# VectorE's written order held two statements longer, to the end of batch 1's first sums

## The chip, the cores and the metric

The kernel runs on one NeuronCore of one Trainium2 chip. Its time is device time of one execution in microseconds (us), and a kernel's time is the median of several executions. A core has TensorE (PE in the profile; its weight loads stand apart as PEld), VectorE (DVE), ScalarE (ACT), GpSimd (POOL) and SyncE (SP), which issues the DMAs here. Each engine works through its own list of instructions in order and waits on semaphores for the others. DVE, ACT and POOL read and write SBUF, PE reads SBUF and writes PSUM, which has 8 banks of 512 float32 per partition.

## What is computed

Everything is float32. Eight batches of 512 tokens, 8 heads of 64, and 32 state rows per head:

```
scores  = x @ state^T / 8;  a  = softmax(scores);   xread = a @ state
scores2 = state @ x^T / 8;  a2 = softmax(scores2);  sread = a2 @ x
y = concat(xread, sread) over tokens            # 544 rows per batch, 512 wide
out = elu(y @ w_in) @ w_out                      # 512 -> 2048 -> 512
```

## The kernel before

**Stages.** A batch's 512 tokens are handled as four 128-row blocks. `batch(b)` (line 847) runs, for `b` from 1 to 7, in two stretches. First come 16 rounds of the first layer: `ffn1` (PE, two matmuls into a bank) and `elu` (two ACT passes, then one DVE instruction that writes `g_all[:, fo]`). Then comes the second layer, `g_all` times `w_out`, as a Strassen product of 2 by 2 blocks (line 572) with seven products. Product P1 is a11 by b11, P2 is a12 by b21. P6, P7 and P5 follow, and two more products are split once more into seven smaller ones (`Second`, line 513). a11 and a12 are the even and odd 128-wide pieces of `g_all` for the first 256 tokens, a21 and a22 those for the other 256.

**Sums.** `whole.sums()` (line 589) is four DVE instructions on 128x1024 elements: two write a21 = a11 - a21 (profile name `g_all<-g_all`), two write s = a22 - a21 (`s<-g_all`). P6 is the first product that reads s, P7 the first that reads the new a21. P1 and P2 read neither.

**The next batch's attention is woven in.** During the last four rounds DVE turns the tokens of batch b+1 (`turn_blocks`, four 128x512 transposes `xT_b<-x_blocks`). After P1's first half PE computes the scores from them and two blocks of `make_m` (`ps<-xT_b,kT`, `ps<-w_in,kT`); DVE, ACT and POOL then do both softmaxes (`attention`, line 709; the first DVE instruction is `top<-ps`). `move_state` (line 359) makes two DVE transposes `a_blocks<-a_s` and then 16 DMAs `aT_s<-a_blocks` of 32 KB from SP. `state_read` (line 374; PE, `ps<-x_sb,aT_s`) needs all of them. It stands in PE's order after the first half of P7. Behind the 16 DMAs SP has two loads of `w_in` and the load of a later batch's tokens.

**Batch 1 alone** also has `weight_sum` in every second round: sums of `w_out` blocks (`t_w<-...`, `w_out<-w_out`, 128x1024), which the Strassen products need. `Second.weights` (line 520) forms further sums of 128x512 (`t<-t_w`, `t_w<-t_w`, `w_out<-w_out`, `w_in<-...`; `t` is the profile's short name for the tile of `second[4]`). They come as hooks after later steps.

**What sets the order.** A scheduler orders each engine's instructions, with estimates of when their inputs are there. The class `InOrder` (line 94) overrides this: while its `on` is true, an instruction issued through it is pinned behind everything issued before it on that engine; while it is false, the scheduler places it. PE and SP are always held. ACT and POOL are held through the first batch. VectorE is held until `vector.on = False` (line 864), which `batch` reaches first in batch 1 and which nothing turns on again. All engine calls go through this helper, so the profile gives one line, L100, for nearly everything, and instructions are told apart by tiles.

Of the kernel before, what the change touches and what calls it, by code (L numbers as in the profile page):

```python
# [25 lines left out]
def kernel(  # L26
# [67 lines left out]
    class InOrder:  # L94
# [10 lines left out]
    tensor, sync, vector, scalar, gpsimd = (  # L105
        InOrder(e) for e in (nc.tensor, nc.sync, nc.vector, nc.scalar, nc.gpsimd)
    )
# [25 lines left out]
    def load_x(b, engines):  # L133
        x_t[b] = xpool.tile([P, R, DM], FP32, name="x_sb")
        x_v = x[b].rearrange("h (p r) d -> p r h d", r=R)
        for r in range(R):
            engines[r % len(engines)].dma_start(
                out=x_t[b][:, r].rearrange("p (h d) -> p h d", d=D), in_=x_v[:, r]
            )

    def load_blocks(b):

        for i in range(2):
            st[b, "blocks", i] = raw = opool.tile([P, 2, R * P], FP32, tag="o", name="x_blocks")
            for j in range(2):
                for k in range(4):
                    x_v = x[b, 2 * (2 * i + j) + k // 2].rearrange(
                        "(q p r) d -> p r q d", q=P // 32, r=R  # L150
                    )
                    sync.dma_start(
                        out=raw[k * 32 : (k + 1) * 32, j].rearrange(
                            "p (r q d) -> p r q d", r=R, d=32
                        ),
                        in_=x_v[:, :, :, k % 2 * 32 : (k % 2 + 1) * 32],
                    )

    def turn_blocks(b, m):

        i, j = divmod(m, 2)
        if j == 0:
            st[b, "xT", i] = work.tile([P, 2, R * P], FP32, tag="w", name="xT_b")
        st[b, m] = st[b, "xT", i][:, j]
        vector.transpose(st[b, m], st[b, "blocks", i][:, j])
# [244 lines left out]
    def fetch_w_in(c, k):  # L410

        for i in range(2):
            sync.dma_start(
                out=w_in[:, 2 * (k + i) : 2 * (k + i) + 2],
                in_=w_in_mem[:, 2 * (c + i) : 2 * (c + i) + 2],
            )

    def make_m(b, c, h=None, first=6):

        c_in = c if b < 2 else c % 2  # L420
        halves = slice(2 * c_in, 2 * c_in + 2) if h is None else slice(2 * c_in + h, 2 * c_in + h + 1)
        assert h is None or b == 0
        st[b, "m", c] = by_state(b, [w_in[:, halves, m] for m in range(NP)], first)

    def copy_m(b, c, g, copy):
        if g == 0:
            m_t[b, c] = mpool.tile([P, G, 512], FP32, name="m_sb")
        copy(out=m_t[b, c][:, g], in_=st[b, "m", c][:, g])
# [20 lines left out]
    def elu(ps, fo):  # L449

        max_part(fo, exp_part(ps), ps)

    def ffn1(b, fo):


        ps = bank(4 + fo % 2 if b == 0 else 3 + (fo + 1) % 3)
        for k in range(G):
            matmul(
                ps,
                m_t[b, fo // 4][:, k, fo % 4 * P : (fo % 4 + 1) * P],  # L460
                st[b, k, "aT"],
                start=(k == 0),
                stop=(k == G - 1),
            )
        return ps
# [37 lines left out]
    def weight_sum(i, half):  # L503

        if i != 3 and half == 0:
            t_w[i] = [
                work.tile([P, FO // 4, DM // 2], FP32, tag="w", name="t_w") for k in range(2)
            ]
        x, y = {1: (b12, b11), 2: (b22, t_w.get(1)), 3: (b22, b12), 4: (b21, t_w.get(2))}[i]
        k = slice(half, half + 1)  # L510
        combine(t_w[i][k], x[k], y[k])
# [197 lines left out]
    def attention(b):  # L709


        def both(*fs):
            for g in range(G):
                for f in fs:
                    f(b, g)

        def s1():

            scores(b)
            for c in range(2):  # L720
                make_m(b, c, first=4 - 2 * c)
            both(column_max, turn_scores, column_exp, row_max, row_subtract, row_exp)
            both(row_sum, row_scale, column_total)
            for c in range(2):
                for g in range(G):
                    copy_m(b, c, g, (scalar.copy, vector.tensor_copy)[g])

        def s2():
            both(turn_tokens)
            move_state(b)  # L730

        nop = lambda: None
        return [lambda: (s1(), s2()), nop, nop, nop, nop, nop, lambda: (state_read(b), keep_read(b))]

    def store(b, i, o_sb):
        rows = out_b[b, 0:S].rearrange("(p r) c -> p r c", r=R)
        sync.dma_start(out=rows[:, 2 * i : 2 * i + 2], in_=o_sb)
# [109 lines left out]
    def batch(b):  # L847
        if b + 1 < B:
            load_blocks(b + 1)
        for fo in range(FO):  # L850
            elu(ffn1(b, fo), fo)
            if fo > 11 and b + 1 < B:
                turn_blocks(b + 1, fo - 12)
            if fo == FO // 4 + 1:
                for c in (2, 3):
                    make_m(b, c, first=6 if c == 2 else 0)
            if FO // 4 + 1 <= fo < FO // 4 + 5:
                c, g = divmod(fo - FO // 4 - 1, G)
                copy_m(b, 2 + c, g, vector.tensor_copy)
            if b == 1 and fo % 2 == 1:  # L860
                weight_sum((1, 2, 4, 3)[fo // 4], fo % 4 // 2)
            if b > 1 and fo == FO // 4 + 2:
                fetch_w_in(0, 0)
        vector.on = False
        nxt = b + 1 < B
        hooks = attention(b + 1) if nxt else [turn_read]
        if nxt and b > 0:
            s1 = hooks[0]
            hooks[0] = lambda: (s1(), fetch_w_in(2, 0))
        if b + 2 < B:  # L870
            hooks += [lambda: load_x(b + 2, [sync])]
        if b == 1:
            hooks += [lambda: second[4].weights(t_w[4]), lambda: second[3].weights(b22)]
            hooks += [lambda: second[5].weights(t_w[1]), lambda: second[7].weights(t_w[3])]
            used = {k: second[k] for k in (4, 3)}
        else:
            used = second
        whole = Strassen(2, used)
        whole.sums()
        for f in whole.steps():  # L880
            f()
            if hooks:
                hooks.pop(0)()
        if not nxt:
            fetch_w_in(2, 2)
        for i in (1, 0):
            store(b, i, whole.o_sb[i])
# [28 lines left out]
    for b in range(1, B):  # L916
        batch(b)
# [31 lines left out]
```

## Time and profile before

| | |
|---|---|
| median of 7 executions | 746.92 us (746.16 to 749.46) |
| the profiled execution | 749.46 us, of which the span is 747.6 us |
| granted TensorE clock | 1.000 |
| PE busy | 723.5 us, 97% |
| DVE busy | 486.1 us, 65% |
| ACT busy | 293.8 us, 39% |
| HBM read and written | 59.24 MB and 13.11 MB |

The profile is of one execution. In its rows "ps<-w_out,g_all 128x256" is an instruction that writes `ps` from `w_out` and `g_all`; "x16" says how many neighbours were merged. Brackets give the idle time of that engine just before and what ended it. Batch 1's first layer ends at about 162 us, its second layer at about 215 us.

### The profile page before, as it was taken

The page shows a single profiled execution, that of the slowest core. Times are in us where ns is not written, and L with a number is a line of the kernel's source. Part 1 is how long each engine was busy: PE and PEld are TensorE (multiplying, and loading weights), DVE is VectorE, ACT ScalarE, POOL GpSimd, SP SyncE. Part 2 cuts the span into 40 slices and gives each one's busy share as a digit, 9 for nine tenths or more (in the row PEclk, how much of TensorE's full clock was granted, in tenths as well). Part 3 has the DMA queues.
Part 4 walks back from the last instruction along what each step waited for, and adds up shares of the span by engine and source line. Part 5 has one row for each costly group of instructions (what it writes and reads, how often), then busy time and mean ns, then how long its engine had stood idle before and what let it go on. Part 6 is the DMA issues. An engine that isn't in the chain of part 4 may idle for free.

```text
span 747.6 us, 11377 instructions
## 1 busy us (share of the span) xinstructions
PE 723.5 (97%) x4472; PEld 502.3 (67%) x4472; DVE 486.1 (65%) x892; ACT 293.8 (39%) x539; POOL 34.4 (5%) x38
## 2 busy tenths in 40 slices
PE   3899999999999999999999999999999999999998
PEld 1634444347874799459944896479746894699886
DVE  1999984699537783677656873787367745556331
ACT  3899974552126410651045213621164106500420
POOL 0200002002000200011000200020002000000000
PEclk9999999999999999999999999999999999999999
DMA  9566910701634053603551154307350403004000
GB/s 282 188 208 223 319 48 1 159 11 17 182 84 142 1 164 90 169 1 80 147 131 67 24 175 106 119 11 188 82 145 1 142 29 140 1 1 141 29 4 25
DMA packets 126366, 76.25 MB, mean 102 GB/s; under 512 B 113768, under 2 KB 114280, under 8 KB 122472
## 3 DMA queue, kind: packets, MB, share of 16 engines
q1 hardware_dynamic: 124004, 74.90, 34.5%
q10 hardware_dynamic: 2308, 0.62, 0.4%
q8 instruction: 35, 0.57, 0.3%
q14 instruction: 19, 0.16, 0.1%
HBM read 59.24 MB, written 13.11 MB: 97 GB/s over the span
## 4 chain that ended last, share of the span: by engine, by line
PE 89%; DVE 5%; DMA 2%; SPq 1%; ACT 1%; issue 1%; POOL 0%; ACTq 0%; DVEq 0%; POOLq 0%
PE ps L100 89%; SPq L100 1%; DMA x_sb<-in_x_dram 1%; DVE w_in L100 1%; DVE g_all L100 1%; DMA raw<-in_moe_w_out_dram 0%; DVE top L100 0%; DVE s L100 0%; DVE w_out L100 0%; ACT e_sb L100 0%; DVE total_t L100 0%; POOL t_sb L100 0%; ACT xT L100 0%; DVE xT_b L100 0%; DVE aT L100 0%
## 5 line engine op out<-in xcount | busy, mean ns | idle before, releaser
L100 PE MATMUL ps<-w_out,g_all 128*128 128x256 f32 (+2 forms) x1088 | 232.5, 366 | 1.6 <-DVE o_sb L100 0.8
L100 PE MATMUL ps<-aT,m_sb 128*128 128x512 f32 x512 | 226.3, 595 | 1.1 <-DVE m_sb L100 0.8
L100 PEld LDWEIGHTS ps<-w_out,g_all 128*128 128x128 f32 x1088 | 176.6, 191 | 54.0 <-issue 37.1
L100 PEld LDWEIGHTS ps<-aT,m_sb 128*128 128x128 f32 x512 | 95.4, 190 | 122.0 <-issue 109.1
L100 ACT ACTIVATE e_sb<-ps 128x512 f32<-128x512 f32 (+1 forms) x144 | 82.6, 573 | 219.9 <-PE ps L100 204.7
L100 DVE SCALAR_TENSOR_TENSOR g_all<-e_sb,ps 128x512 f32<-128x512 f32 (+1 forms) x144 | 94.3, 657 | 101.0 <-ACT e_sb L100 100.4
L100 DVE TENSOR_TENSOR o_sb<-o_sb,ps 128x128 f32<-128x128 f32 (+2 forms) x170 | 52.7, 310 | 75.2 <-PE ps L100 73.5
L100 ACT ACTIVATE e_sb<-e_sb 128x512 f32<-128x512 f32 (+1 forms) x144 | 87.6, 608 | 4.6
L100 PE MATMUL ps<-t_w,s 128*128 128x256 f32 (+1 forms) x480 | 88.8, 339 | 0.0
L100 PEld LDWEIGHTS ps<-t_w,s 128*128 128x128 f32 x480 | 77.6, 191 | 8.1 <-DVE o_sb L100 0.2
L100 ACT COPY o_sb<-ps 128x512 f32<-128x512 f32 (+2 forms) x52 | 20.6, 424 | 152.2 <-PE ps L100 144.5
L100 ACT ACTIVATE raw<-raw 128x512 f32<-128x512 uint32 x64 | 43.8, 685 | 1.0
L100 DVE TENSOR_TENSOR s<-s,g_all 128x512 f32<-128x512 f32 (+1 forms) x36 | 32.2, 897 | 15.9 <-PE ps L100 15.5
L100 POOL TENSOR_TENSOR t_sb<-t_sb,top_t 128x512 f32<-128x512 f32 x16 | 16.7, 1048 | 519.7 <-DVE top_t L100 519.7
L100 DVE TENSOR_TENSOR g_all<-g_all,s 128x512 f32<-128x512 f32 (+1 forms) x36 | 32.1, 892 | 9.6 <-PE ps L100 9.6
L100 PE MATMUL ps<-w_in,kT 64*32 64x512 f32 (+1 forms) x576 | 34.0, 547 | 1.1 <-ACT a_s L100 1.1
L100 DVE TENSOR_TENSOR g_all<-g_all 128x512 f32<-128x512 f32 (+1 forms) x36 | 32.2, 895 | 0.5
L100 DVE TENSOR_TENSOR s<-g_all 128x512 f32<-128x512 f32 (+1 forms) x36 | 31.6, 883 | 1.1 <-DMA aT_s<-a_blocks 0.8
L100 PE MATMUL ps<-t_w,g_all 128*128 128x128 f32 (+1 forms) x240 | 32.1, 282 | 0.0
L100 PE MATMUL ps<-w_in,s 128*128 128x128 f32 x240 | 31.2, 277 | 0.0
L100 PEld LDWEIGHTS ps<-t_w,g_all 128*128 128x128 f32 x240 | 29.8, 192 | 0.5
L100 PEld LDWEIGHTS ps<-w_in,s 128*128 128x128 f32 x240 | 28.7, 192 | 0.6 <-DVE o_sb L100 0.3
(86 smaller groups left out, 557.0 us busy)
## 6 DMA issues: line engine op xcount, KB each, us to landing
w_in<-w_in_mem SPq DMA_DIRECT2D x26, 1024.0 KB, 6.0
raw<-in_moe_w_in_dram SPq DMA_DIRECT2D x16, 512.0 KB, 4.8
raw<-in_moe_w_out_dram SPq DMA_DIRECT2D x16, 512.0 KB, 4.2
out_dram<-o_sb SPq DMA_DIRECT2D x16, 512.0 KB, 2.9
x_sb<-in_x_dram SPq DMA_DIRECT2D x30, 256.0 KB, 4.7
x_blocks<-in_x_dram SPq DMA_DIRECT2D x96, 64.0 KB, 2.4
w_in_mem<-w_in SPq DMA_DIRECT2D x4, 1024.0 KB, 8.4
aT_s<-a_blocks SPq DMA_DIRECT2D x96, 32.0 KB, 1.9
```

The source lines that it names most:

```text
L100: ins = getattr(self.engine, name)(*args, **kw)
```

## The change

`vector.on = False` moves from the end of the rounds to behind `whole.sums()`. Between the two places VectorE is issued nothing but the four sums, since the hooks and products are only set up there. So in batch 1 the four sums are pinned behind all that was issued on VectorE before them: the last `elu`, the last transpose, the last `weight_sum`. In later batches `vector.on` is false already. The instructions are the same; only places in the order differ.

```diff
@@ def batch(b)
             if b > 1 and fo == FO // 4 + 2:
                 fetch_w_in(0, 0)
-        vector.on = False
         nxt = b + 1 < B
         hooks = attention(b + 1) if nxt else [turn_read]
         if nxt and b > 0:
@@
             used = second
         whole = Strassen(2, used)
         whole.sums()
+        vector.on = False
         for f in whole.steps():
             f()
             if hooks:
```

The built order of VectorE's instructions at this place, before and changed (sizes are elements per partition):

```
before                              changed
(round 8)                           (round 8)
g_all<-g_all     1024               -
...                                 ...
xT_b<-x_blocks    512  first        xT_b<-x_blocks    512  first
-                                   t<-t_w,t          512
elu of round 13                     elu of round 13
xT_b<-x_blocks    512  second       xT_b<-x_blocks    512  second
w_out<-w_out     1024               w_out<-w_out     1024
elu of round 14                     elu of round 14
xT_b<-x_blocks    512  third        xT_b<-x_blocks    512  third
elu of round 15                     elu of round 15
g_all<-g_all     1024               t<-t_w,t          512
s<-g_all         1024 x2            t_w<-t_w          512
t<-t_w,t          512               w_out<-w_out      512
                                    w_in<-w_out       512
xT_b<-x_blocks    512  fourth       xT_b<-x_blocks    512  fourth
w_out<-w_out     1024               w_out<-w_out     1024
-                                   g_all<-g_all     1024 x2
-                                   s<-g_all         1024 x2
top<-ps (softmax begins)            top<-ps (softmax begins)
...                                 ...
a_blocks<-a_s     512 x2            a_blocks<-a_s     512 x2
```

Between `top` and the second `a_blocks` the order is the same. Behind it, the small weight sums that stood there before are gone where they were moved forward, and `o_sb<-o_sb,ps` of P2 stands before the last `aT` transpose. On ACT the second copy `m_sb<-ps` moves ahead of the first softmax step and the copy of P1's result (`o_sb<-ps`) ahead of the second. The orders of PE, POOL and SP are unchanged.

## The prediction

> **What bounds the kernel now.** I read the page's busy times first, then the chain of work that ended last, then the timelines of PE, DVE and SP around the end of batch 1's rounds, where alone the order changes.
>
> ```profile
> PE 723.5 (97%) x4472; PEld 502.3 (67%) x4472; DVE 486.1 (65%) x892; ACT 293.8 (39%) x539; POOL 34.4 (5%) x38
> ```
>
> PE is busy 97%, so time is won or lost only where PE is held up. The chain shows where that happens in batch 1:
>
> ```profile
> 163.09 0.62 DVE xT_b L100
> 163.71 1.70 DVE g_all L100 x2
> 165.42 0.07 DVE s L100
> ...
> 166.47 1.22 DVE s L100
> 167.69 0.60 DVE t L100
> 168.29 0.63 DVE xT_b L100
> 168.92 0.04 issue
> 168.97 400.46 PE ps L100 x2596
> ```
>
> Before 168.97 the chain lies on DVE: sums and a small weight sum stand ahead of the fourth `xT_b`, without which the last scores cannot start. From there PE runs 400 us without a hold. PE's timeline gives the hold, and the place where the softmax's result is needed next:
>
> ```profile
> 165.56 1.07 PE L100 MATMUL ps<-xT_b,kT 64*32 64x512 f32 x12
> 168.97 0.62 PE L100 MATMUL ps<-xT_b,kT 64*32 64x512 f32 x2 [2.33 <-DVE xT_b L100]
> ...
> 171.66 10.63 PE L100 MATMUL ps<-w_out,g_all 128*128 128x256 f32 x48
> 182.12 7.07 PE L100 MATMUL ps<-t_w,s 128*128 128x256 f32 x32
> 189.03 3.62 PE L100 MATMUL ps<-w_out,g_all 128*128 128x256 f32 x16
> 192.58 1.10 PE L100 MATMUL ps<-x_sb,aT_s 128*32 128x64 f32 x64
> ```
>
> PE idles 2.33 us for `xT_b`. At 192.58 `state_read` starts with no idle time. Its input arrives just before, as SP and DVE show:
>
> ```profile
> 179.13 0.66 DVE L100 STREAM_TRANSPOSE a_blocks<-a_s 128x512 f32<-128x512 f32 x1
> ...
> 192.58 0.69 DVE L100 TENSOR_TENSOR s<-g_all 128x512 f32<-128x512 f32 x1 [0.83 <-DMA aT_s<-a_blocks]
> ```
>
> ```profile
> 179.85 10.43 SPq L100 DMA_DIRECT2D aT_s<-a_blocks  x16
> 190.38 1.03 SPq L100 DMA_DIRECT2D w_in<-w_in_mem  x2
> ```
>
> SP issues the 16 transfers from 179.85 to 190.28, 0.06 us behind the last `a_blocks` (179.79). At a median of 1.9 us to landing the last is there at 192.18. A DVE sum that waits for the same transfers starts at 192.58. So `state_read` has 0 to 0.4 us of slack, against about 3 us in batch 2 (issue ends 271.09, landed 273.0, `state_read` at 276.12). That is what the change works on.
>
> **The change part by part.** Starts on DVE follow each other by 0.60 us for 128x512, 0.63 behind a transpose, 1.13 for 128x1024 (163.63, 164.21, 165.34, 167.60, 168.20 in DVE's timeline).
>
> *Round 8: a sum of 1.13 us goes.* It stood at 148.90 in a stretch where DVE ran behind ACT; by 156.65 before and changed meet again, since that `elu` waits for ACT until 156.61. PE does not idle between 149.04 and 165.56. Worth 0, hidden by PE's own work.
>
> *Round 13: a 128x512 sum comes in* at 159.61. The next `elu` starts at 160.21 instead of 160.08; the rest of the 0.60 fills an idle 0.39 and a wait. The last `elu` slips from 163.63 to 163.76. P1's first half (162.02 to 165.56) reads up to round 14, the eighth of its matmuls at about 163.6, and that `elu` ends at 163.2. No cost.
>
> *Ahead of the fourth transpose* three sums of 1.13 and one of 0.60 go, 3.99 us; four of 0.60 come, 2.40. The transpose starts at 163.76 + 0.58 + 2.40 = 166.74 instead of 168.20, so PE resumes 1.46 us sooner, at 167.51. This gain is PE's until `state_read`: P1's second half, P2, P6 and half of P7 need nothing that is late. P6's s is ready at 173.0 and P6 starts at 180.66; ACT copies P1's bank at about 175.1, behind the first softmax step, with P1 done at 173.74.
>
> *Behind the fourth transpose*, ahead of `top`, now stand the `w_out` sum (1.10) and all four sums (4.52): 166.74 + 0.63 + 1.10 + 4.52 = 172.99, against 170.04. So the softmax starts 2.95 us later although PE's scores are there sooner.
>
> *The softmax itself is as before.* From `top` to the end of the second `a_blocks` it took 9.75 us (170.04 to 179.79), and 9.75 again in batch 2 (250.87 to 260.62). ACT's and POOL's steps hang on DVE's and move with them. `a_blocks` ends at 182.74.
>
> *SP, all 16 DMAs counted:* 0.06 to start, 10.43 to issue, 1.9 to land: 195.13. PE starts between there and 0.4 later, by the slack above; I take 195.33, the middle. PE is at `state_read` at 192.58 - 1.46 = 191.12, idles 4.2 us and starts 2.75 us later than before. The two `w_in` loads behind the transfers and the token load, which waits for `state_read`, move with it; batch 2 reads them tens of us later.
>
> *Work behind `state_read`.* DVE reaches P2's `o_sb` sum at 182.74 and frees the bank by 183.4; P7 needs it at 187.57. The two sums that P5 needs end at about 191; P5 would start at 200. The small weight sums moved forward no longer stand behind `a_blocks`. So DVE makes no second hold, and little can be won back: from 192.58 on PE's only idle time is 0.81 us (at 594.64, for `o_sb`). Were all of it to go, the sum would be 1.9 us.
>
> *The clock after a longer idle stretch* is not shown by the trace. Bounds: no cost as after 2.33 us idle, where the next 48 matmuls took 10.63 us, 0.221 each, as do the 32 at 182.12; or as in the start of the kernel, after sparse work:
>
> ```profile
> 16.46 1.96 PE L100 MATMUL ps<-xT,kT 64*32 64x512 f32 x16 [1.67 <-ACT xT L100]
> 18.35 4.69 PE L100 MATMUL ps<-ident 128*128 128x128 f32 x28
> ```
>
> The same 16 scores take 1.09 us in batch 2 and 28 such `ident` matmuls 3.39 us at 30.97, so 0.87 + 1.30 = 2.2 us were lost, with a granted clock of 1.00 in both places. I take 0, since the gap lies in dense work, nearer to the first row; 2.2 stays the upper end.
>
> [...]
>
> **Sum:** -1.46 + 4.2 = +2.75 us. The profiled execution would go from 749.46 to 752.2. It is the slowest of the seven shown, 2.54 over the median, so for the median I add the same to 746.92: 749.7 us.
>
> **Rivals.**
> 1. *The clock drops after the idle stretch.* For it: the two slow rows above; against it: 2.33 us did nothing. 746.92 + 2.75 + 2.2 = 751.9 us.
> 2. *The gain stays: faster.* `state_read` is not held, because `aT_s` lands by 191.1. The softmax would have to start by 168.9, that is, the 5.62 us of sums behind the transpose would have to delay it by nothing. It decides above a landing of 192.6. For it: all that PE needs up to there is early. Against it: DVE works in order, and every step up to the landing has a row. 746.92 - 1.46 = 745.5 us.
> 3. *No change.* The loss meets the gain, if the chain from `top` to `state_read` has over 2 us that can shrink, for instance in ACT's and POOL's waits. Against it: 9.75 us in two batches alike, and 16 equal issues of 0.65. 746.9 us. That the change does nothing is excluded by the built order.
> 4. *A second hold on DVE*, such as P2's `o_sb` sum releasing P7's bank late. It would need over 4 us more delay than I find; every us beyond costs one. 750.7 us for one.
>
> **How the numbers follow.** Forecast 0.65, clock 0.17, faster 0.06, no change 0.07, second hold 0.05. The forecast's own range is 748.8 (1.9 us) to 749.9 (2.95 us). For 8 in 10 I leave out the faster case and part of the unchanged one and go up past the clock case; the seven executions alone spread over 3.3 us, so the range is 747.8 to 752.6. A change under 0.2% (1.5 us) cannot be told from none in this kernel. Faster 0.06; same 0.08 (no change, and a small part of the forecast won back); slower 0.86.
>
> **What would show it.** In the changed profile PE's idle time before the last scores falls from 2.33 to about 0.9 us; `top` starts at about 173.0; `a_blocks` ends at about 182.7; `state_read` shows an idle time of about 4.2 us put down to `aT_s<-a_blocks` and starts at about 195.3; P7's second half behind it keeps 0.22 us per matmul (slow clock: 0.4). The prediction is wrong if `top` still starts near 170, if `state_read` has no idle time before it, or if 2 us are won back after it.

## The result, and the profile after

The changed kernel is slower. Its median is 751.52 us (17 executions, 748.09 to 752.46), against 748.1 us for the kernel before in the same comparison (45 executions). The ratio is 1.004, with a 95% interval of 1.003 to 1.005: about +3.0 us, where +2.75 was predicted (the two medians themselves lie 3.4 us apart). The profiled execution of after took 750.23 us with a span of 748.4 us and a mean granted clock of 0.995; the one of before took 749.46 with a span of 747.6 and a clock of 1.000.

The two profiles cannot be subtracted as they stand, since after reached batch 1's P1 2.36 us earlier (159.66 instead of 162.02) by differences in work that the change does not touch: its first scores, behind the start-up loads, already begin at 13.58 instead of 16.46. So I count from the start of P1's first half in batch 1 to the start of the same half in batch 2. That took 84.10 us before (162.02 to 246.12) and 87.58 after (159.66 to 247.24): +3.48 us. The same interval of batches 2 to 5 is equal to within 0.02 us (79.59, 79.75, 79.53, 79.67 after). All of the loss is in batch 1. From batch 2's P1 to the end after took 0.3 us less than before (748.4 - 247.24 against 747.6 - 246.12), with PE's one wait for `o_sb` in that stretch down from 0.8 to 0.5 us.

PE's busy time, from the page of after, grew by 3.5 us with the same number of matmuls, so some of them ran slower:

```profile
PE 727.0 (97%) x4472; PEld 505.2 (68%) x4472; DVE 485.2 (65%) x892; ACT 294.3 (39%) x539; POOL 34.4 (5%) x38
```

The chain of waits of after, between 159 and 195 us (start, duration, what):

```profile
164.42 0.62 DVE xT_b L100
165.04 1.10 DVE w_out L100
166.15 2.27 DVE g_all L100 x2
168.42 2.27 DVE s L100 x2
170.69 0.60 DVE top L100
...
179.76 0.59 DVE a_blocks L100
180.40 0.63 SPq L100
...
189.58 0.61 SPq L100
190.24 1.91 DMA aT_s<-a_blocks
192.14 0.14 issue
192.28 3.04 PE ps L100 x60
```

Before, this chain left DVE at the fourth `xT_b` and then ran on PE for 400 us. Now it goes on along DVE, through the four held sums into the softmax, then through SP's 16 issues and the last landing, and comes to PE only with `state_read`. The duration of the DMA in the chain, 1.91 us, is counted from the start of the last issue at 190.24.

PE's timeline of after shows both ends of the trade:

```profile
163.20 1.08 PE L100 MATMUL ps<-xT_b,kT 64*32 64x512 f32 x12
165.10 0.62 PE L100 MATMUL ps<-xT_b,kT 64*32 64x512 f32 x2 [0.82 <-DVE xT_b L100]
...
185.17 3.62 PE L100 MATMUL ps<-w_out,g_all 128*128 128x256 f32 x16
188.71 0.31 PE L100 MATMUL ps<-x_sb,aT_s 128*32 128x64 f32 x4
189.67 0.27 PE L100 MATMUL ps<-x_sb,aT_s 128*32 128x64 f32 x2 [0.65 <-DMA aT_s<-a_blocks]
192.28 1.88 PE L100 MATMUL ps<-x_sb,aT_s 128*32 128x64 f32 x58 [2.34 <-DMA aT_s<-a_blocks]
194.09 4.36 PE L100 MATMUL ps<-w_out,g_all 128*128 128x256 f32 x16
198.28 7.07 PE L100 MATMUL ps<-t_w,s 128*128 128x256 f32 x32
```

The hold ahead of the last scores fell from 2.33 to 0.82 us. In exchange `state_read` waits twice, 0.65 and 2.34 us. Six of its 64 matmuls run as the first blocks land, and the other 58 wait for the last. Behind the wait the work is slower than before: those 58 take 1.88 us (all 64 took 1.10 before), and the 16 matmuls of P7's second half take 4.36 us instead of 3.72.

The table of stretches says why (columns: stretch, its length, busy time and count of PE, PEld, DVE, ACT and POOL, the granted PE clock, the DMA share, GB/s). After:

```profile
180.00:190.00 10.00, 9.29 (x47) 7.68 (x45) 9.14 (x12) 0.59 (x1) 0.96 (x1) 1.00 0.26 43
190.00:195.00 5.00, 2.72 (x60) 2.49 (x61) 1.99 (x3) 0.63 (x2) 0.00 (x0) 0.70 0.70 211
195.00:196.00 1.00, 1.00 (x5) 0.82 (x5) 0.00 (x0) 0.00 (x0) 0.00 (x0) 0.79 0.95 361
196.00:200.00 4.00, 4.00 (x20) 3.52 (x19) 1.38 (x2) 0.59 (x1) 0.00 (x0) 1.00 1.09 321
```

The granted clock is 0.50 from 192.0, still inside the wait, to 195.4 us (the finer stretches are shown at the end). In the profile of before it is 1.00 throughout batch 1. So two things were added: a wait, and a slow clock behind it.

Steps of the two kernels, counted from the start of P1's first half (162.02 before, 159.66 after), in us:

| step | before | after | difference | predicted |
|---|---|---|---|---|
| last scores resume | 6.95 | 5.44 | -1.51 | -1.46 |
| `top` starts | 8.02 | 10.94 | +2.92 | +2.95 |
| second `a_blocks` ends (start of SP's first issue less 0.06) | 17.77 | 20.68 | +2.91 | +2.95 |
| `state_read` (its bulk) starts | 30.56 | 32.62 | +2.06 | +2.75 |
| P7's second half starts | 31.59 | 34.43 | +2.84 | +2.75 |
| P5 starts | 35.15 | 38.62 | +3.47 | +2.75 |

Up to SP the prediction holds to 0.05 us. Then `state_read` starts 0.7 us sooner than predicted, and the slow clock takes that back and 0.7 us more.

### The profile page after: what moved, and what is told of

Read it like the earlier page. It is cut to its first block, busy times and chain, and to the rows that moved or that the text cites. A ratio compares the mean times of both kernels' runs of the same rounds, so it can differ in the third digit from the quotient of the medians.

```text
span 748.4 us, 11377 instructions
## 1 busy us (share of the span) xinstructions
PE 727.0 (97%) x4472; PEld 505.2 (68%) x4472; DVE 485.2 (65%) x892; ACT 294.3 (39%) x539; POOL 34.4 (5%) x38
## 4 chain that ended last, share of the span: by engine, by line
PE 80%; DVE 12%; SPq 3%; ACT 2%; DMA 1%; issue 1%; POOL 0%; ACTq 0%; DVEq 0%; POOLq 0%
PE ps L100 80%; DVE w_in L100 4%; DVE w_out L100 3%; SPq L100 3%; DVE g_all L100 2%; DMA x_sb<-in_x_dram 1%; DVE top L100 1%; DVE s L100 1%; DMA aT_s<-a_blocks 1%; ACT e_sb L100 0%; DVE t_sb L100 0%; POOL t_sb L100 0%; DVE m_sb L100 0%; DVE top_t L100 0%; DVE t_w L100 0%
```

## The experiments

The theory by now: the gain at the last scores is real (1.5 us), the four sums ahead of `top` delay `aT_s`, and `state_read` waits for it. The clock part (rival 1) and the wait are to be told apart. The rivals to be excluded: that the loss comes from something else that moved, such as the small weight sums, and that the slow clock is an accident of one execution. The first four kernels share their executions of before, whose median there was 747.87 us.

**The wait filled with matmuls.** On the changed kernel, PE is given 13 `ident` matmuls (26 in the profile) ahead of `state_read`, so that it does not idle. Their result is not used.

```diff
+        if b == 1:
+            read_hook = hooks[6]
+            def warm_read():
+                for _ in range(13):
+                    matmul(bank(4)[:, :P], ident, ident, start=True, stop=True)
+                read_hook()
+            hooks[6] = warm_read
```

> The changed kernel with 13 products of the identity with itself (26 matmuls on PE, into a bank nobody reads) ahead of batch 1's state_read, in the time in which PE would wait for aT_s. Theory: the loss has two parts, a later state_read (2.1 us) and a slow clock behind the idle stretch (about 1 us on average, 1.4 us in the profiled execution). Then the filled kernel keeps the first part alone: state_read's bulk starts as late as before relative to P1, the granted clock is 1.00 from 190 us on, P7's second half takes 3.6 us instead of 4.36, ratio to the kernel before about 1.0028 instead of 1.004. Rival (the slow stretch is an accident of that execution, the stall alone is the loss): ratio unchanged at 1.004.

Measured: 749.28 us (748.38 to 750.38), ratio 1.0021 [1.0011, 1.0032]. PE's timeline of this kernel:

```profile
188.26 3.06 PE L100 MATMUL ps<-ident 128*128 128x128 f32 x26
191.25 0.31 PE L100 MATMUL ps<-x_sb,aT_s 128*32 128x64 f32 x6
191.92 1.05 PE L100 MATMUL ps<-x_sb,aT_s 128*32 128x64 f32 x58 [0.36 <-DMA aT_s<-a_blocks]
192.90 3.72 PE L100 MATMUL ps<-w_out,g_all 128*128 128x256 f32 x16
```

The last block lands when it did before the fill: the 58 matmuls start 32.62 us after P1 (191.92 less 159.30), exactly as in after. But they take 1.05 us instead of 1.88, and the granted clock of the stretch is 1.00:

```profile
190.00:195.00 5.00, 4.64 (x86) 4.07 (x86) 2.05 (x4) 0.63 (x2) 0.00 (x0) 1.00 0.74 239
```

The interval from P1 to P1 is 86.11 us, +2.01 over before: that is the price of the late data alone, net of the gain at the scores. The other 1.47 us of after's +3.48 are the clock's. The ten executions have mean clocks of 0.998 to 1.000, those of after 0.993 to 1.000. One thing was not foreseen: the interval from batch 5 to batch 6 grew to 80.54 us (+0.88), with a wait of PE for `o_sb` there.

**`state_read` later in PE's order.** On the changed kernel `state_read` and the two steps behind it move two steps back, from between P7's halves to between P5's, so that the data is there first.

```diff
+            read_hook, load_hook, w4_hook = hooks[6:9]
+            hooks[6:9] = [lambda: None] * 2 + [lambda: (read_hook(), load_hook(), w4_hook())]
```

> The changed kernel with batch 1's state_read (and the token load behind it) two steps later in PE's order, between the two halves of P5, that is 7.1 us later. Theory: aT_s has landed 3.6 us before PE comes there, so there is no idle stretch and no slow clock, and of the change only its gain is left, PE's wait for the fourth xT_b of 0.8 instead of 2.3 us: ratio 0.998 (-1.5 us). Rival (the loss is DVE work elsewhere, or the softmax result is needed by something else first): ratio stays at 1.002 to 1.004.

Measured: 745.71 us (744.89 to 746.81), ratio 0.9973 [0.9964, 0.9981]: faster than before. PE's timeline of this kernel:

```profile
164.47 0.62 PE L100 MATMUL ps<-xT_b,kT 64*32 64x512 f32 x2 [0.81 <-DVE xT_b L100]
...
195.00 1.10 PE L100 MATMUL ps<-x_sb,aT_s 128*32 128x64 f32 x64
```

The wait ahead of `state_read` is gone, all 64 matmuls run in 1.10 us, and the interval is 82.59 us: 1.51 less than before, the gain at the scores to the hundredth. So the change loses by this one wait and what follows from it, and by nothing else.

**The same move on the kernel before,** as the control: there `state_read` did not wait, so nothing should come of it.

> The kernel before with batch 1's state_read two steps later, as a control for the run above. Theory: before, aT_s landed about 1 us ahead of PE, so nothing is gained: ratio 1.000 (within 0.0005). Rival (state_read was held in the kernel before, too): faster by what it was held, 0.999 or less.

Measured: 748.14 us (746.01 to 749.72), ratio 1.0000 [0.9987, 1.0013]; the interval is 84.10 us as before, and the wait of 2.3 us for `xT_b` stays. The late place alone is worth nothing. Only the "about 1 us ahead" of the expectation is off: in the profile of before the last transfer was there at 192.3, about 0.3 us ahead of PE (see below).

**Only part of the sums ahead of `top`.** On the changed kernel the sum of a21's first half is left to the scheduler, and the holding is turned on again behind it. In DVE's timeline this sum goes back to 146.10 and the s sum that reads it to 161.41, ahead of the fourth transpose (165.54); the second a21 sum stands at 167.27 ahead of `top` (168.40), and its s sum at 169.00, just behind it. So one sum instead of four stands between the transpose and `top`.

```diff
         def sums(self):
-            combine(self.a21, self.a11, self.a21)
+            held = vector.on
+            combine(self.a21[1:], self.a11[1:], self.a21[1:])
+            vector.on = False
+            combine(self.a21[:1], self.a11[:1], self.a21[:1])
+            vector.on = held
```

> The changed kernel with only one of the two a21 sums (the one over the second half of g_all's pieces) held behind what was issued before; the other goes back to round 8 and its s sum ahead of the fourth transpose. In the built order the fourth xT_b stands 0.1 us later than in the kernel before, top behind one 128x1024 sum (+1.1 us), and another 128x1024 sum stands between the first two softmax steps (+1.1 us), so a_blocks ends about 2.3 us later. Theory: about 1 us of that is taken up by the time that aT_s landed early, so state_read starts 1.3 us later, the idle stretch of 1.2 us is too short for the clock, which stays at 1.00: ratio 1.0018. Rival (every us of softmax delay costs one): 1.003. Rival (a shorter stall slows the clock, too): 1.003 with a granted clock under 1.

Measured: 749.04 us (747.76 to 750.28), ratio 1.0014 [1.0004, 1.0025]. The ratio is near the expected one, but in the profile the loss lies elsewhere. PE's timeline of this kernel, and one line of its table of stretches:

```profile
162.77 1.08 PE L100 MATMUL ps<-xT_b,kT 64*32 64x512 f32 x12
166.30 0.69 PE L100 MATMUL ps<-xT_b,kT 64*32 64x512 f32 x2 [2.46 <-DVE xT_b L100]
...
166.80 3.96 PE L100 MATMUL ps<-w_in,kT 64*32 64x512 f32 x26
...
191.61 1.10 PE L100 MATMUL ps<-x_sb,aT_s 128*32 128x64 f32 x64
```

```profile
166.00:176.00 10.00, 9.70 (x61) 5.79 (x62) 10.00 (x21) 4.25 (x9) 2.09 (x2) 0.83 0.01 2
```

Here the slow clock (0.83 over ten us) followed the wait of 2.46 us ahead of the last scores: 26 `w_in` matmuls took 3.96 us, which take 2.30 us in the kernel with the late `state_read`. PE then came to `state_read` late enough not to wait. The interval is 85.94 us, +1.84, of which 1.66 are those 26 matmuls. The expectation that the clock stays at 1.00 failed. This suggests that the wait of 2.33 us that the kernel before has at this place can cost the clock too.

**That wait filled in the kernel before.** Nine `ident` matmuls stand ahead of the last group of scores of batch 2, and in a second kernel six. Their result is not used.

```diff
         for m in range(NP):
+            if fill and m == NP - 1:
+                for _ in range(9):
+                    matmul(bank(1)[:, :P], ident, ident, start=True, stop=True)
```

> The kernel before with 9 products of the identity with itself (18 matmuls, 2.1 us, into a bank nobody reads) on PE ahead of batch 1's last scores, in the 2.33 us in which PE waits for the fourth xT_b. The run that held one sum showed the clock at 0.83 behind a wait of that length, and executions of the kernel before show mean clocks of 1.000, 0.998 and 0.995, the slower the lower. Theory: this wait, too, costs clock in part of the executions; filled, the wait stays as long, but the mean clock stays at 0.998 or above, the executions lie closer together, and the ratio is 0.9985 to 0.9993. Rival (the low clocks of the kernel before come from its first 100 us alone): ratio 1.000 and clocks as before.

> The kernel before with 6 instead of 9 products of the identity ahead of batch 1's last scores (12 matmuls, 1.4 us of the 2.33 us wait). The first such run kept the clock up but lost 1.2 us in batch 5, where SP took 11.6 instead of 10.4 us to issue its 16 transfers and PE waited 0.97 us for o_sb. Theory: if batch 5 is as in the kernel before (80 us from P1 to P1, no such wait), the clock gain shows: ratio 0.998 to 0.9995 with clocks of 0.998 and above. If batch 5 is longer again, its 0.9 to 1.2 us hide the gain: ratio 1.000. Rival (a low clock behind the wait costs nothing): ratio 1.000 with batch 5 as before.

Measured with nine: 748.26 us (747.19 to 749.55), ratio 1.0006 [0.9996, 1.0016]. With six: 747.92 us (747.13 to 748.33), ratio 0.9994 [0.9985, 1.0002]. The clock part of the expectation held: mean clocks of 0.997 to 1.000 in all 23 executions, where before, on the same chips, had 0.995 in 7 of 17 and in 8 of 23. But no gain in time came of it, so the expectation failed. Batch 1's interval is that of before (84.11 and 84.10 us). What would take the gain away is batch 5: its interval to batch 6 is 80.90 and 80.85 us instead of 79.66, with PE waits of up to 1.0 us for `o_sb`. PE's waits in the kernel with six (total, times, longest):

```profile
PE ps L100 <- DVE o_sb L100: 1.7, 2, 0.9
```

All three kernels with added matmuls show this loss in batch 5, and none of the others. The first guess, that SP's 16 issues take longer there (11.64 us with nine), fell with the second kernel, where they took 10.40 us. The cause stays open.

**The small weight sums held too.** On the kernel with the late `state_read`, the hooks behind it are issued with VectorE held, so that their sums stay in written order and don't stand ahead of the fourth transpose.

```diff
+            def held(f):
+                vector.on = True
+                f()
+                vector.on = False
+            hooks[8:] = [lambda f=f: held(f) for f in hooks[8:]]
```

> The changed kernel with state_read two steps later and with the small weight sums of batch 1 (second[4], [3], [5], [7]) held in written order, too, so that they come after the products in whose steps they are issued and none stands ahead of the fourth xT_b. Theory: the fourth xT_b follows the last elu at once, PE has no wait there (0 instead of 0.8 us), the softmax starts about 0.4 us later than in the kernel before, state_read finds its input: ratio 0.996 (-2.3 us of wait and some clock). Rival (the late weight sums hold up the two split products): ratio 0.9975 or more, with PE waiting for t, t_w or b.

> The fastest kernel so far (small weight sums of batch 1 held, state_read late) with state_read back in its old place behind P7's first half. Theory: the fourth xT_b comes as early (no wait ahead of the last scores), but PE is then at state_read 27.2 us after P1's start while aT_s lands after about 30.0: an idle stretch of about 2.8 us, state_read's bulk 0.5 us sooner than in the kernel before, and some slow clock behind it: ratio 0.998 to 1.000 (the held sums also take away 0.8 us of PE's waits ahead of P1), 2 to 4 us slower than with the late state_read. Rival (the late place of state_read does nothing once the sums are held): ratio 0.995 as with it.

Measured with the late `state_read`: 743.84 us (743.1 to 744.79), ratio 0.9947 [0.9935, 0.9959], about 4.0 us less than before and the fastest kernel of all. PE's timeline:

```profile
161.99 1.09 PE L100 MATMUL ps<-xT_b,kT 64*32 64x512 f32 x16
162.88 1.92 PE L100 MATMUL ps<-w_in,kT 64*32 64x512 f32 x32
...
192.55 1.10 PE L100 MATMUL ps<-x_sb,aT_s 128*32 128x64 f32 x64
```

PE waits neither ahead of the scores nor ahead of `state_read`, and the interval is 81.60 us (-2.50). A wait of 0.76 us for `m_sb` at 149 us, which before had, is gone as well. It gained more than was expected.

The second text is for the same kernel with `state_read` left at its old place: 747.64 us (746.32 to 749.33), ratio 0.9985 [0.9977, 0.9994], and an interval of 86.11 us. PE's timeline and one stretch:

```profile
187.03 0.59 PE L100 MATMUL ps<-x_sb,aT_s 128*32 128x64 f32 x6
189.95 1.45 PE L100 MATMUL ps<-x_sb,aT_s 128*32 128x64 f32 x58 [2.33 <-DMA aT_s<-a_blocks]
191.33 4.95 PE L100 MATMUL ps<-w_out,g_all 128*128 128x256 f32 x16
```

```profile
190.00:195.00 5.00, 5.00 (x69) 4.25 (x70) 4.57 (x7) 0.63 (x2) 0.00 (x0) 0.66 0.92 359
```

The bulk of `state_read` starts 30.12 us after P1, a little sooner than before (30.56). But with no wait at the scores PE arrives sooner still, waits 2.33 us, and the clock falls (0.66 over five us). So in this kernel the place of `state_read` must go back when PE's earlier wait is taken away.

**The changed kernel again,** to see whether the slow clock was an accident.

> The changed kernel once more, on the chip of the two runs above, to see in a second profile whether the two parts of its loss stand as in the first. Theory: ratio 1.004; the bulk of state_read starts 2.1 us later relative to P1's first half than in the kernel before, behind an idle stretch of about 3.5 us; the mean clock of most executions is 0.993 to 0.995, against 0.995 to 1.000 before. Rival: the low clock of the first profile was an accident, and this one shows 1.00 at 190 to 196 us.

Measured: 750.97 us (750.0 to 753.08), ratio 1.0044 [1.0029, 1.006]. The profiled execution has the same steps (scores resume at 5.44 us, the 58 matmuls start at 32.62 us) and a longer slow stretch. PE's timeline and two stretches:

```profile
193.31 1.89 PE L100 MATMUL ps<-x_sb,aT_s 128*32 128x64 f32 x58 [2.33 <-DMA aT_s<-a_blocks]
195.12 5.69 PE L100 MATMUL ps<-w_out,g_all 128*128 128x256 f32 x16
```

```profile
190.00:195.00 5.00, 2.02 (x62) 1.81 (x60) 1.43 (x3) 0.32 (x1) 0.00 (x0) 0.73 0.55 138
195.00:200.00 5.00, 5.00 (x19) 3.97 (x14) 1.51 (x3) 0.31 (x1) 0.00 (x0) 0.59 1.03 371
```

The interval is 88.91 us, 2.80 over that of the filled kernel. The slow clock is not an accident, and its price in one execution is 1.47 or 2.80 us.

## Why the prediction was right

*-1.46 us at the last scores: right.* 1.51 us measured, and with the late `state_read` the whole interval fell by just that.

*Nothing lost in rounds 8 and 13, and nothing behind `state_read` in other engines' work: right.* From PE's last wait in batch 1's rounds, 0.76 us for `m_sb` in both profiles, to P1 it took 12.98 us before (149.04 to 162.02) and after (146.68 to 159.66). The intervals of the other batches did not move, and the late `state_read` gave the full gain; a loss elsewhere would have remained.

*`top` +2.95 us, softmax as before, SP 0.06 + 10.43 us: right* to 0.05 us.

*"At a median of 1.9 us to landing": 0.6 us too much for the changed kernel, and right for the kernel before by luck.* I added 1.9 us to the end of the last issue; the traces count it from the start. In the kernel before this went unnoticed, because its last two transfers, which start at 189.0 and 189.7, took 3.1 and 2.6 us instead of 1.9. Times from start to landing of these transfers in batch 1, before and then after:

```profile
DMA to landing us min/median/max: 1.9/1.9/3.1
DMA to landing us min/median/max: 1.9/1.9/2.0
```

So before, the data was there at 192.3, near the 192.18 that I had worked out, and the slack of 0 to 0.4 us was about 0.3 us. After, the last transfer landed 1.91 us behind its start, at 192.15. SP's first issue moved by 2.91 us, the last landing took 0.7 us less, and PE followed it 0.14 us sooner: 2.06 us. The term of 4.2 us of stall should have been 3.5; the two waits measured 2.99 us, with six matmuls done ahead of the second. Why the last two were slower stays open. All four kernels with the sums in the order of before show it (longest landing 2.7 to 3.1 us), the others do not (2.0 at most).

*The clock, "I take 0": wrong.* Rival 1, with a chance of 0.17, happened: the profile of after lost 1.47 us by it, the second one 2.80. Over all executions it is about 1 us net: by the ratio the time went up by 3.0 us, and the late data explains 2.0. It is net because before seems to lose some clock at its own wait in part of its executions (mean clocks of 0.995 in 7 of 17 and 8 of 23, against none in the 23 with that wait filled). My reason was that 2.33 us of idle time in this place had done nothing. That was one execution. The same place with 2.46 us idle was followed by a clock of 0.50 for 3.40 us in the kernel with part of the sums held, and other executions of before show mean clocks of 0.995 and 0.998. The upper end of 2.2 us rested on rows near 16 and 18 us with a granted clock of 1.00, but the trace's clock records begin only at 21.1 us, so that clock was not measured there. The 0.4 us per matmul that I named for a slow clock was an estimate that no row of before showed; after shows 0.43 us from start to start inside its slow stretch (194.25, 194.68 and 195.11, in P7's second half) and 0.22 behind it.

So the size came out right by luck: a stall 0.7 us too long stood in for a clock cost of about 1 us that was left out. As a time, 751.52 us lies above the forecast's own 748.8 to 749.9 and next to the 751.9 of rival 1; 1.2 us of that is the kernel before, whose median over 45 executions is 748.1 and not the 746.92 that I started from. The direction, the place and the mechanism of the wait were right for the reasons given. Rivals 2, 3 and 4 are excluded: `state_read` was held, no more than 0.3 us was won back, and no second hold on DVE shows.

*From what idle length on the clock falls is not shown.* The longest uninterrupted waits that a slow clock followed were 2.33 to 2.46 us. The stretch from the last 128*128 matmul to the end of the wait was about 3.5 us long (188.71 to 192.28 in after, 162.77 to 166.30 in the kernel with part of the sums held), filled only in part by matmuls on tiles 32 wide. But in the profile of before the same stretch took 3.41 us (165.56 to 168.97), with a wait of 2.33 us in it, and the clock stayed at 1.00; and in the second profile of after the clock fell at 192.31, only 2.5 us after the last 128*128 matmul (186.20 + 3.62). So no length measured here tells the executions with a slow clock from those without. What such narrow work does to the clock was not tested by itself.

## What to carry to other kernels

An order that is held longer moves everything behind it: follow the pinned work to what it stands ahead of (here a softmax, 16 DMAs and a read on PE), not only to what it frees. When an early wait on PE is removed, the consumers of long chains further on arrive early too, so move them back in PE's order first; the same held sums cost 3.0 us with `state_read` in its old place and won 2.0 us two steps later. And a wait on a dense PE had two prices here, its own length (2.33 to 2.46 us) and the slow clock behind it (1.47 and 2.80 us in the two profiles of after, 1.66 in the kernel with part of the sums held). The profile of before, with a wait of 2.33 us and a clock of 1.00, was no proof that such a wait is free.

## What the runs showed of the hardware

**In these profiles the slow clock came in pieces of 3.4 us at a granted clock of 0.50.** Finer stretches, of after, the kernel with part of the sums held, the one with the early read and the weights held, and the second profile of after:

```profile
192.00:195.41 3.41, 3.13 (x61) 2.81 (x62) 1.99 (x3) 0.63 (x2) 0.00 (x0) 0.50 0.95 322
166.73:170.13 3.40, 3.40 (x34) 0.92 (x20) 3.40 (x4) 0.55 (x1) 0.00 (x0) 0.50 0.03 5
190.45:193.86 3.41, 3.41 (x43) 2.79 (x33) 3.31 (x6) 0.63 (x2) 0.00 (x0) 0.50 0.97 387
192.31:199.13 6.82, 5.82 (x68) 4.88 (x69) 2.17 (x4) 0.63 (x2) 0.00 (x0) 0.50 0.90 320
```

The granted clock is 0.50 for 3.4 us in the first three and for 6.8 us, twice as long, in the last. By that, a piece takes away 1.7 us of full-speed time (3.41 times 0.50, an estimate). That is 0.0023 of the span, which fits the mean clocks of most executions, 1.000, 0.998, 0.995 and 0.993, as none to three pieces. After's table of stretches of 20 us shows its two:

```profile
20.00:40.00 20.00, 17.31 (x164) 11.88 (x164) 18.27 (x37) 16.37 (x32) 2.35 (x2) 0.91 0.67 207
180.00:200.00 20.00, 17.01 (x129) 14.52 (x128) 12.51 (x17) 1.80 (x4) 0.96 (x1) 0.91 0.57 156
```

The first, near the start of the kernel (0.50 from 24.75 to 28.16), cost almost nothing. After is 2.88 us ahead of the profile of before at the first scores (13.58 against 16.46), only 1.35 us ahead at the `ident` matmuls right behind the piece (29.62 against 30.97), but 2.81 us again soon after (`ps<-aT,m_sb`, 40.51 against 43.32). The second is the one behind `state_read`. How many there are differs from execution to execution: the same kernel showed one piece at `state_read` in one profile and two in the other.

**The last transfer's landing time ran beside its own issue.** The last of the 16 transfers landed 1.91 us after its issue began, so only 1.3 us after the issue of about 0.6 us had ended. The time to landing is not the same in every kernel: the same transfer took 2.6 us in the profile of before.
